# Turning the third and fourth chunks' first layer norm on VectorE by way of DRAM, instead of on TensorE

## The chip, the cores and the metric

The kernel runs on one core of one Trainium2 chip. The metric is the device time in microseconds (us) of one execution; lower is better. Engines are named as in the profile: PE (TensorE, matmuls), PEld (its weight loads), ACT (ScalarE), DVE (VectorE), POOL (GpSimd), SP (SyncE, which issues all the DMAs here).

## What is computed

One transformer block with conditioned layer norms, in float32: 2048 tokens of 512 features, 32 heads of 16 in a linear attention, and a bilinear gated unit of 1376 hidden features.

```python
mod = (_silu(c) @ w_mod).reshape(c.shape[0], 6, 1, -1)
sa, ca, ga, sb, cb, gb = (mod[:, 0], mod[:, 1], mod[:, 2], mod[:, 3], mod[:, 4], mod[:, 5])
h = _layernorm(x, axis=-1) * (1 + ca) + sa
x = x + ga * _A_ref(h, A_wqkv, A_wo)          # linear attention
h = _layernorm(x, axis=-1) * (1 + cb) + sb
x = x + gb * _B_ref(h, B_w_gate, B_w_up, B_w_down)   # ((h w_gate) * (h w_up)) w_down
```

In the attention, phi(t) is t + 1 for t > 0 and exp(t) otherwise, plus 1e-6; the keys' phi(k) enters a sum over all tokens (phi(k) times v, and phi(k) alone, here called z), which all queries then read.

## The kernel before

The 2048 tokens are four chunks of four tiles; a tile is 128 tokens by 512 features, a chunk `ch` has the tiles 4 ch to 4 ch + 3. Every float32 matmul is made of three: each operand is split into a high part (a copy in the matmul's own format, made on ACT, sometimes on DVE) and a low part (what is left, a subtraction on DVE or POOL), and the products high-high, high-low and low-high are added up in PSUM. One product of a 128-token tile with a 512x512 weight is so twelve matmuls with 512 columns: four slices `k` of the features, three each.

The order of the instructions is written by hand; each engine works through its own list in order. The change lies in the first half, the key loop (`for i in range(NT)`, 16 passes, `ch, j = divmod(i, 4)`). Pass `i` issues, for PE: the key projection of tile i + 2 (`proj(i + 2, wk)`, L207 to L209), in passes 3, 4, 6 and 7 also a query projection (`proj(q, wq)`), and `t_tile(i)` (L373 to L375), which adds tile i's part to the sum over tokens. For the other engines it issues: `k_split_x(i + 1)` and `k_split(i + 1)`, the high and low parts of the normalised tile (`xh`, `xl`) and of phi of its keys (`kh`, `kl`) that the next pass's `t_tile` reads; `k_phi(i + 2)`, which makes phi out of the projection (two ACT instructions, L337 and L338, one DVE instruction, L341); `z_add`; and a part of side work (`extra[i]`): the splits of the value weights, the modulation vectors (`mod_load`, `mod_part`), the splits of the output weights `wo_s`.

A projection needs the chunk's layer norm transposed, features on the partitions. Before, chunk `ch + 1` is made so while chunk `ch` runs: statistics in the last two passes of the chunk before (DVE, L242, L243; the power on POOL, L263), the normalised tiles (`xhat`, ACT, L272), then in passes j = 0 and j = 1 the transposes (`turn_x`: sixteen times 128x128 on PE against an identity, in two groups of eight a chunk, L293), and the reading of PSUM with scale and shift (`modulated`, ACT, L305) with the high part cast on DVE (L313) and the low part (L316). For the third and fourth chunks these groups stand in passes 4, 5, 8 and 9, each in the middle of `t_tile`.

After the loop the sum over tokens is scaled (L655, L656), split (L194, L195), multiplied with the value weights and then with the output weights (`w_out`).

In the second half the kernel already moves tiles through DRAM and turns them on DVE: `move_out` and `move_in` (one write of 128x512, four reads of 32x4x128), `turn_v` (L736), and for the last layer norm `flip` (L901) and `flipped` (L907). A DVE transpose turns blocks of 32x32; the DRAM pass regroups the blocks so that the whole is transposed.

All tiles of 128x512 come from one pool of 94 buffers; PSUM has eight banks, four of which (`bank`) serve the projections and the turns.

Of the kernel before, what the change touches and what calls it, by code (L numbers as in the profile page):

```python
# [8 lines left out]
F32 = mybir.dt.float32  # L9
F32R = mybir.dt.float32r  # L10
AF = mybir.ActivationFunctionType
ALU = mybir.AluOpType
AX = mybir.AxisListType

P = 128
NB = 94
BL = 32
NQ = P // BL
# [6 lines left out]
def tile_adaln_block(  # L25
# [12 lines left out]
    nc = tc.nc  # L38
    ctx.enter_context(tc.manual_schedule())
    _, S, D = x.shape  # L40
    F = w_gate.shape[1]
    KD = D // P
    NJ = 4
    CH = NJ * P
    NCH = S // CH
# [22 lines left out]
    def f32(ap):  # L68
        return ap.bitcast(F32)
# [3 lines left out]
    def T(p, tag, shape=(P, D), dt=F32, bufs=None):  # L73
        cnt[0] += 1
        return p.tile(list(shape), dt, tag="t" if p is tiles else tag, name=f"{tag}_{cnt[0]}", bufs=bufs)

    def B(tag, shape=(P, D), dt=F32):

        return T(tiles, tag, shape, dt)
# [4 lines left out]
    def bank():  # L84
        return T(ps_w, "bank")
# [20 lines left out]
    wide = consts.tile([P, NJ, D], F32, name="wide")  # L106
# [59 lines left out]
    def mod_col(acc, ps):  # L166

        for b in range(KD):
            nc.tensor.matmul(ps[:, b:b + 1], acc[:, b * P:(b + 1) * P], ones[:, 0:1], start=True, stop=True)
        return ps  # L170

    def col_out(v, ps, add):
        t = consts.tile([P, KD], F32, name=f"col{v}")
        nc.vector.tensor_scalar(t, ps[:, :KD], add, None, op0=ALU.add)
        return t
# [17 lines left out]
    def split(src, h, l, low=None):  # L193
        nc.scalar.activation(h, src, AF.Copy)  # L194
        (low or nc.vector).tensor_tensor(l, src, f32(h), op=ALU.subtract)  # L195

    def split_raw(raw, shape=(P, D), low=None):
        h = B("w", shape, F32R)
        l = B("w", shape, F32R)
        split(raw, h[:raw.shape[0]], l[:raw.shape[0]], low)  # L200
        return h, l
# [17 lines left out]
    def by_row(x):  # L219
        return x.rearrange("p (q s i) -> p s q i", q=NQ, i=BL)  # L220
# [96 lines left out]
                self.t[k] = (h, l)  # L317


    NT = NCH * NJ  # L320
    norm = [Norm(xts[0])]
    wk, wq, wv = [], [], []
    kx, phk, phq, q_ps = {}, {}, {}, {}

    def proj(i, w, of=bank):

        ch, j = divmod(i, NJ)
        ps = of()
        rows = w is wq and i not in FLIPPED
        product(ps.rearrange("p (s q i) -> p s q i", q=NQ, i=BL) if rows else ps,  # L330
                [(cut(norm[ch].t[k], j * P, (j + 1) * P), tuple(by_row(x) for x in w[k]) if rows else w[k])
                 for k in range(KD)])
        return ps
# [9 lines left out]
    def k_split_x(i):  # L343
        ch, j = divmod(i, NJ)
        kx[i] = [B("xh", dt=F32R), B("xl", dt=F32R)]
        split(norm[ch].n[j], *kx[i])

    def k_phi(i, ps):
        phi = B("phi")
# [11 lines left out]
    def k_split(i):  # L361
        h, l = B("kh", dt=F32R), B("kl", dt=F32R)
        phi = phk[i]
        nc.scalar.activation(h, phi, AF.Identity, bias=eps_phi)
        nc.vector.scalar_tensor_tensor(l, phi, EPS_PHI, f32(h), op0=ALU.add, op1=ALU.subtract)
        kx[i] += [h, l]

    def t_tile(i, *ks):
        xh, xl, kh, kl = kx[i]
        first, last = i == 0, i == NT - 1  # L370
        for k in ks:
            a, b = k * P, (k + 1) * P
            nc.tensor.matmul(tacc[k], xh[:, a:b], kh, start=first, stop=False)  # L373
            nc.tensor.matmul(tacc[k], xl[:, a:b], kh, start=False, stop=False)  # L374
            nc.tensor.matmul(tacc[k], xh[:, a:b], kl, start=False, stop=last)  # L375
# [6 lines left out]
    def q_b(i):  # L382
        phi_b(q_ps.pop(i), phq[i])
# [28 lines left out]
    ca = col_out(1, ps_ca, 1.0)  # L412
# [3 lines left out]
    sa = consts.tile([P, KD], F32, name="col0")  # L416
# [47 lines left out]
    nx = Norm(xts[1])  # L464
# [31 lines left out]
    rows, cols = {}, {}  # L496
    accs = {}

    raw_m, raw_o, wo_s = {}, [], []

    def mod_load(*vs):
        raw_m.update({v: load_mod(v) for v in vs})

    def mod_part(v, *ks):
        if 0 in ks:
            accs[v] = B("f")
        mod_acc(accs[v], raw_m[v], ks)
# [6 lines left out]
             9: lambda: (mod_part(2, 2, 3), mod_load(4)),  # L514
             10: lambda: (pairs.update({2: split_raw(accs[2], low=nc.gpsimd)}), mod_part(3, 0, 1, 2), raw_o.extend(load(wo_v[k], "raw") for k in range(2))),
             11: lambda: (mod_part(3, 3), mod_part(4, 0, 1), rows.update({2: mod_row(2, pairs[2])}), raw_o.extend(load(wo_v[k], "raw") for k in range(2, KD))),
             12: lambda: (mod_part(4, 2, 3), wo_s.extend(split_raw(x) for x in raw_o[:2]), cols.update({3: col_out(3, mod_col(accs[3], bank()), 0.0)}), mod_load(5)),
             13: lambda: (mod_part(5, 0, 1, 2), wo_s.extend(split_raw(x) for x in raw_o[2:]), cols.update({4: col_out(4, mod_col(accs[4], bank()), 1.0)})),
             14: lambda: (mod_part(5, 3),)}
    pairs = {}  # L520
    q_at = {3: 0, 4: 1, 6: 2, 7: 3}
    ahead = {2: k_ps[2], 3: k_ps[3]}
    turn_at = {4 * ch + j: (ch + 1, 2 * j, 2 * j + 1) for ch in range(1, NCH - 1) for j in range(2)}
    turn_at.update({1: (1, 0, 1), 2: (1, 2, 3)})
    for i in range(NT):
        ch, j = divmod(i, NJ)
        done = 0
        if i > 2:
            ahead[i + 2] = proj(i + 2, wk) if i + 2 < NT else proj(i + 6 - NT, wq)
        if i in q_at:  # L530
            qps = proj(q_at[i], wq)
        def turn_x():
            to, *ks = turn_at[i]
            nx.transpose(*ks)
            nx.modulated(ca, sa, *ks, cast=nc.vector)
            norm[to:] = [nx]

        fresh = i > 0 and ch + 1 < NCH and j == 0
        if i == 2:
            turn_x()  # L540
            wq.extend(split_blocks(r) for r in raw_q)
        if fresh:
            nx.xhat(2)
        if 0 < i < NT - 1:
            k_split_x(i + 1)
        if fresh:
            nx.xhat(3)
        if 0 < i < NT - 1:
            k_split(i + 1)
        if i in turn_at and i != 2:  # L550
            t_tile(i, 0, 1)
            done = 2
            turn_x()
        if i == 2:
            t_tile(i, *range(KD))
            done = KD
            ahead[i + 2] = proj(i + 2, wk)
        if ch + 2 < NCH and j == 2:
            nx2 = Norm(xts[ch + 2])
            nx2.stats(0, 1)  # L560
        if ch + 2 < NCH and j == 3:
            nx = nx2
            nx.stats(2, 3)
            nx.rstd_of()
            nx.nmr_of()
            nx.xhat(0, 1)
        if i + 2 < NT:
            k_phi(i + 2, ahead.pop(i + 2))
        else:
            q_a(i + 6 - NT, ahead.pop(i + 2))  # L570
            q_b(i + 6 - NT)
        if i in q_at:
            q_a(q_at[i], qps)
            q_b(q_at[i])
        if i + 1 < NT:
            z_add(i + 1)
        if i == NT - 2:
            pairs["z"] = split_raw(zacc, low=nc.gpsimd)
        if i == NT - 1:
            zps = row_sum(pairs["z"])  # L580
            zb = consts.tile([P, D], F32, name="zb")
            nc.scalar.activation(zb, zps, AF.Identity, bias=eps_z)
            zq = B("z")
            nc.gpsimd.tensor_copy(zq.rearrange("p (q s i) -> p q s i", q=NQ, i=BL), by_block(zb))
        t_tile(i, *range(done, KD))
        if i in extra:
            extra[i]()
    ga, sb, cb = rows[2], cols[3], cols[4]
# [64 lines left out]
    for k in range(KD):  # L653
        f = B("n")
# [62 lines left out]
    moved = {}  # L717

    def move_out(*tiles):

        for i in tiles:
            moved[i] = tc.dram_tile([P, D], F32, name=f"moved_{i}")
            nc.sync.dma_start(moved[i], phq.pop(i))

    def move_in(*tiles):

        for i in tiles:
            v = moved[i].rearrange("(m i) (q c) -> q i m c", i=BL, c=P)
            moved[i] = B("u")
            for q in range(NQ):  # L730
                nc.sync.dma_start(moved[i][q * BL:(q + 1) * BL].rearrange("i (m c) -> i m c", c=P), v[q])

    def turn_v(i):

# [163 lines left out]

    def flip(ch, *js):
        for j in js:  # L900
            nc.vector.transpose(wide[:, j].rearrange("p (m s i) -> p m s i", m=NQ, i=BL),  # L901
                                blocks.pop((ch, j)).rearrange("p (m s i) -> p m s i", m=NQ, i=BL))

    def flipped(ch, *ks):
        for k in ks:
            f = B("f")
            nc.scalar.activation(f.rearrange("p (x i) -> p x i", i=BL),  # L907
                                 wide.rearrange("p j (m s i) -> p (j m) s i", m=NQ, i=BL)[:, :, k],
                                 AF.Identity, scale=cb[:, k:k + 1], bias=sb[:, k:k + 1])
            blocks[ch, "f", k] = f  # L910

    stowed, blocks = {}, {}

# [518 lines left out]
```

## Time and profile before

| | |
|---|---|
| three runs | 553.96, 554.49, 555.14 us; median 554.49 |
| the profiled execution | 554.37 us, span of its instructions 552.7 us |
| busy share of the span | PE 99%, PEld 81%, DVE 68%, ACT 53%, POOL 37% |
| turns on PE in the whole run (L293) | 80 of 128x128, 10.4 us busy |
| DMA | 58.28 MB, mean 105 GB/s |

Times in the rows are microseconds from the span's start, means and durations in an instruction's row are marked there; a matmul's length in a row includes the time in which it overlaps the next one, so the pace is read from the starts. "xN" is a count of merged instructions; a bracket names the engine's idle time before the row and what ended it.

### The profile page before, as it was taken

The page shows a single profiled execution, that of the slowest core. Times are in us where ns is not written, and L with a number is a line of the kernel's source. Part 1 is how long each engine was busy: PE and PEld are TensorE (multiplying, and loading weights), DVE is VectorE, ACT ScalarE, POOL GpSimd, SP SyncE. Part 2 cuts the span into 40 slices and gives each one's busy share as a digit, 9 for nine tenths or more (in the row PEclk, how much of TensorE's full clock was granted, in tenths as well). Part 3 has the DMA queues.
Part 4 walks back from the last instruction along what each step waited for, and adds up shares of the span by engine and source line. Part 5 has one row for each costly group of instructions (what it writes and reads, how often), then busy time and mean ns, then how long its engine had stood idle before and what let it go on. Part 6 is the DMA issues. An engine that isn't in the chain of part 4 may idle for free.

```text
span 552.7 us, 7324 instructions
## 1 busy us (share of the span) xinstructions
PE 547.0 (99%) x2488; PEld 449.2 (81%) x2488; DVE 373.6 (68%) x610; ACT 291.7 (53%) x539; POOL 203.4 (37%) x204
## 2 busy tenths in 40 slices
PE   8999999999999999999999999999999999999997
PEld 7788888888888878878888888877888888888886
DVE  7896968986887886778776576985444444434434
ACT  3695856646476667566684545454443444444110
POOL 2000000102003201057596666766666546446200
PEclk9999999999999999999999999999999999999999
DMA  8900203320503205845545071690434222200004
GB/s 284 387 15 2 76 20 103 108 77 1 157 2 133 96 5 186 267 145 135 160 111 155 0 230 38 216 322 2 133 116 132 59 57 59 58 20 0 1 0 152
DMA packets 58373, 58.28 MB, mean 105 GB/s; under 512 B 7328, under 2 KB 38304, under 8 KB 58336
## 3 DMA queue, kind: packets, MB, share of 16 engines
q1 hardware_dynamic: 58336, 57.83, 33.2%
q8 instruction: 19, 0.31, 0.2%
q14 instruction: 18, 0.15, 0.1%
HBM read 42.60 MB, written 15.20 MB: 105 GB/s over the span
## 4 chain that ended last, share of the span: by engine, by line
PE 99%; DVE 0%; issue 0%
PE bank L1030 33%; PE acc L766 7%; PE acc L1110 6%; PE acc L1111 6%; PE acc L1112 6%; PE bank L207 5%; PE bank L209 5%; PE bank L208 5%; PE acc L375 3%; PE acc L374 3%; PE acc L373 3%; PE bank L849 2%; PE bank L851 2%; PE bank L850 2%; PE acc L146 2%; PE bank L293 2%
## 5 line engine op out<-in xcount | busy, mean ns | idle before, releaser
L1030 PE MATMUL bank<-h,w 128*128 128x512 f32 (+1 forms) x798 | 184.7, 390 | 0.0
L1030 PEld LDWEIGHTS bank<-h,w 128*128 128x128 f32 (+1 forms) x798 | 148.4, 186 | 33.4 <-ACT bank L1035 0.7
L1035 ACT ACTIVATE bank<-bank 128x512 f32<-128x512 f32 (+1 forms) x38 | 22.2, 583 | 139.6 <-PE bank L1030 139.5
L836 DVE TENSOR_TENSOR x<-acc,x 128x512 f32<-128x512 f32 (+1 forms) x73 | 48.8, 682 | 48.4 <-PE acc L1112 47.7
L1016 POOL TENSOR_TENSOR w<-raw,w 128x256 fp32r<-128x256 f32 (+3 forms) x38 | 40.9, 1077 | 91.0 <-ACT w L1009 91.0
L1111 PE MATMUL acc<-w,kh 128*128 128x512 f32 (+2 forms) x154 | 59.6, 387 | 0.0
L1110 PE MATMUL acc<-w,kh 128*128 128x512 f32 (+2 forms) x154 | 59.6, 387 | 0.0
L1112 PE MATMUL acc<-w,kl 128*128 128x512 f32 (+2 forms) x154 | 59.5, 386 | 0.0
L263 POOL TENSOR_TENSOR rstd<-ve,half 128x4 f32<-128x4 f32 (+1 forms) x10 | 11.0, 1103 | 121.8 <-DVE ve L262 69.6
L195 POOL TENSOR_TENSOR w<-raw,w 128x512 fp32r<-128x512 f32 (+1 forms) x25 | 35.1, 1409 | 52.2 <-ACT w L194 47.3
L1016 POOL TENSOR_TENSOR w<-t,w 128x512 fp32r<-128x512 f32 (+1 forms) x38 | 49.2, 1318 | 0.0
L195 DVE TENSOR_TENSOR kl<-u,kh 128x512 fp32r<-128x512 f32 (+1 forms) x38 | 26.4, 736 | 30.6 <-ACT kh L194 30.6
L207 PE MATMUL bank<-w,h 128*128 128x512 f32 x104 | 40.9, 394 | 0.0
L209 PE MATMUL bank<-w,h 128*128 128x512 f32 x104 | 40.6, 391 | 0.0
L208 PE MATMUL bank<-w,h 128*128 128x512 f32 x104 | 40.6, 390 | 0.0
L766 PE MATMUL acc<-w,xh 128*128 128x512 f32 x120 | 37.4, 393 | 0.0
L1089 DVE TENSOR_TENSOR u<-bank,u 128x512 f32<-128x512 f32 (+1 forms) x19 | 13.1, 691 | 31.6 <-PE bank L1030 25.1
L1110 PEld LDWEIGHTS acc<-w,kh 128*128 128x128 f32 (+1 forms) x154 | 28.9, 188 | 6.0
L1112 PEld LDWEIGHTS acc<-w,kl 128*128 128x128 f32 (+1 forms) x154 | 28.9, 188 | 5.9
L1111 PEld LDWEIGHTS acc<-w,kh 128*128 128x128 f32 (+1 forms) x154 | 28.9, 188 | 5.9
L998 POOL TENSOR_TENSOR t<-raw,t 128x256 f32<-128x256 f32 (+1 forms) x34 | 25.9, 761 | 1.4
L766 PEld LDWEIGHTS acc<-w,xh 128*128 128x128 f32 x120 | 22.2, 188 | 4.6
(211 smaller groups left out, 1116.5 us busy)
## 6 DMA issues: line engine op xcount, KB each, us to landing
raw<-in_w_mod_dram SPq DMA_DIRECT2D x24, 256.0 KB, 3.7
raw<-in_B_w_down_dram SPq DMA_DIRECT2D x20, 256.0 KB, 3.2
raw<-in_B_w_gate_dram SPq DMA_DIRECT2D x36, 128.0 KB, 3.4
raw<-in_B_w_up_dram SPq DMA_DIRECT2D x36, 128.0 KB, 3.4
x<-in_A_x_dram SPq DMA_DIRECT2D x16, 256.0 KB, 5.4
out_dram<-x SPq DMA_DIRECT2D x15, 256.0 KB, 2.6
raw<-in_A_wqkv_dram SPq DMA_DIRECT2D x12, 256.0 KB, 5.4
moved<-h SPq DMA_DIRECT2D x12, 256.0 KB, 2.1
```

Of the source, the lines that this page charges most:

```text
L195: (low or nc.vector).tensor_tensor(l, src, f32(h), op=ALU.subtract)
L207: nc.tensor.matmul(ps, ah, bh, start=i == 0, stop=False)
L208: nc.tensor.matmul(ps, ah, bl, start=False, stop=False)
L209: nc.tensor.matmul(ps, al, bh, start=False, stop=i == n - 1)
L766: nc.tensor.matmul(yps[i], x, y, start=False, stop=k == KD - 1 and x is al, skip_group_check=True)
L836: nc.vector.tensor_tensor(xt[:, a:b], dn[j][:, a:b], xt[:, a:b], op=ALU.add)
L998: sub = lambda out, x, y: (on or nc.gpsimd).tensor_tensor(out, x, y, op=ALU.subtract)
L1016: sub = lambda out, x, y: (on or nc.gpsimd).tensor_tensor(out, x, f32(y), op=ALU.subtract)
L1030: mm = lambda x, y, **kw: nc.tensor.matmul(ps, x[:, k], y, skip_group_check=True, **kw)
L1110: nc.tensor.matmul(ps, hh[:, a:b], dh[:n, c:d], start=i == 0, stop=False)
L1111: nc.tensor.matmul(ps, hh[:, a:b], dl[:n, c:d], start=False, stop=False)
L1112: nc.tensor.matmul(ps, hl[:, a:b], dh[:n, c:d], start=False, stop=i == len(hs) - 1)
```

## The change

The first layer norm of chunks 2 and 3 (the third and fourth) no longer goes over PE. In passes 3 and 7 all four tiles of the third and of the fourth chunk are normalised in regrouped order (`xhat_blocks`) and written to DRAM; in passes 4 and 8 each is read back in four pieces; in passes 5 and 9 DVE turns the four tiles into the constant buffer `wide`, and ACT makes a row of each k with scale and shift, followed by the high and low parts. For the third chunk, two of the four high parts are cast on DVE; for the fourth, all are on ACT. `k_split_x` reads the regrouped tiles of these chunks with strides. In pass 6 the query projection comes before the key projection. The four splits of the output weights move from passes 12 and 13 to 14 and 15. The helpers `lift_out`, `lift_in`, `lift_turn` and `lift_row` also take the place of the same instructions in the second half.

```diff
+    LIFTED = (2, 3)
+
+    def lift_out(name, x):
+        to = tc.dram_tile([P, D], F32, name=name)
+        nc.sync.dma_start(to, x)
+        return to
+
+    def lift_in(of):
+        v = of.rearrange("(m i) (q c) -> q i m c", i=BL, c=P)
+        u = B("u")
+        for q in range(NQ):
+            nc.sync.dma_start(u[q * BL:(q + 1) * BL].rearrange("i (m c) -> i m c", c=P), v[q])
+        return u
+
+    def lift_turn(j, u):
+        nc.vector.transpose(wide[:, j].rearrange("p (m s i) -> p m s i", m=NQ, i=BL),
+                            u.rearrange("p (m s i) -> p m s i", m=NQ, i=BL))
+
+    def lift_row(k, scale, shift):
+        f = B("f")
+        nc.scalar.activation(f.rearrange("p (x i) -> p x i", i=BL),
+                             wide.rearrange("p j (m s i) -> p (j m) s i", m=NQ, i=BL)[:, :, k],
+                             AF.Identity, scale=scale[:, k:k + 1], bias=shift[:, k:k + 1])
+        return f
+
+    def lift_parts(k, f, cast=True):
+        h, l = B("h", dt=F32R), B("h", dt=F32R)
+        if k % 2 and cast:
+            nc.vector.tensor_copy(h, f)
+        else:
+            nc.scalar.activation(h, f, AF.Copy)
+        nc.vector.tensor_tensor(l, f, f32(h), op=ALU.subtract)
+        return h, l
...
     def k_split_x(i):
         ch, j = divmod(i, NJ)
         kx[i] = [B("xh", dt=F32R), B("xl", dt=F32R)]
-        split(norm[ch].n[j], *kx[i])
+        if ch not in LIFTED:
+            split(norm[ch].n[j], *kx[i])
+            return
+        x = by_row(norm[ch].n[j])
+        h, l = (t.rearrange("p (s q i) -> p s q i", q=NQ, i=BL) for t in kx[i])
+        nc.scalar.activation(h, x, AF.Copy)
+        nc.vector.tensor_tensor(l, x, f32(h), op=ALU.subtract)
...
-             12: lambda: (mod_part(4, 2, 3), wo_s.extend(split_raw(x) for x in raw_o[:2]), cols.update({3: col_out(3, mod_col(accs[3], bank()), 0.0)}), mod_load(5)),
-             13: lambda: (mod_part(5, 0, 1, 2), wo_s.extend(split_raw(x) for x in raw_o[2:]), cols.update({4: col_out(4, mod_col(accs[4], bank()), 1.0)})),
-             14: lambda: (mod_part(5, 3),)}
+             12: lambda: (mod_part(4, 2, 3), cols.update({3: col_out(3, mod_col(accs[3], bank()), 0.0)}), mod_load(5)),
+             13: lambda: (mod_part(5, 0, 1, 2), cols.update({4: col_out(4, mod_col(accs[4], bank()), 1.0)})),
+             14: lambda: (mod_part(5, 3), wo_s.extend(split_raw(x) for x in raw_o[:2])),
+             15: lambda: wo_s.extend(split_raw(x) for x in raw_o[2:])}
...
-    turn_at = {4 * ch + j: (ch + 1, 2 * j, 2 * j + 1) for ch in range(1, NCH - 1) for j in range(2)}
-    turn_at.update({1: (1, 0, 1), 2: (1, 2, 3)})
+    turn_at = {1: (1, 0, 1), 2: (1, 2, 3)}
     for i in range(NT):
         ch, j = divmod(i, NJ)
         done = 0
+        up = ch + 1 if 0 < ch < NCH - 1 else None
+        if i == 6:
+            qps = proj(q_at[i], wq)
         if i > 2:
             ahead[i + 2] = proj(i + 2, wk) if i + 2 < NT else proj(i + 6 - NT, wq)
-        if i in q_at:
+        if i in q_at and i != 6:
             qps = proj(q_at[i], wq)
+        if up and j == 0:
+            lifts = [lift_in(x) for x in lifts]
+        if up and j == 1:
+            lift_turn(0, lifts[0])
...
-        if fresh:
-            nx.xhat(2)
         if 0 < i < NT - 1:
             k_split_x(i + 1)
-        if fresh:
-            nx.xhat(3)
-        if 0 < i < NT - 1:
             k_split(i + 1)
+        if up and j == 1:
+            lift_turn(1, lifts[1])
...
-            nx.xhat(0, 1)
+            nx.xhat_blocks(0, 1)
...
+        if ch + 2 < NCH and j == 3:
+            nx.xhat_blocks(2, 3)
+            lifts = [lift_out(f"first_{ch}_{n}", x) for n, x in enumerate(nx.n)]
...
         t_tile(i, *range(done, KD))
+        if up and j == 1:
+            lift_turn(2, lifts[2])
+            lift_turn(3, lifts[3])
+            for k in range(KD):
+                nx.t[k] = lift_parts(k, lift_row(k, ca, sa), cast=up == 2)
+            norm[up:] = [nx]
```

More of the change, by code (lines that the diff above doesn't have):

```diff
@@ L536, in turn_x @@
             norm[to:] = [nx]
-        fresh = i > 0 and ch + 1 < NCH and j == 0
         if i == 2:
@@ L721, in move_out @@
         for i in tiles:
-            moved[i] = tc.dram_tile([P, D], F32, name=f"moved_{i}")
-            nc.sync.dma_start(moved[i], phq.pop(i))
+            moved[i] = lift_out(f"moved_{i}", phq.pop(i))
     def move_in(*tiles):
         for i in tiles:
[L728 to L731, printed above, removed]
+            moved[i] = lift_in(moved[i])
     def turn_v(i):
@@ L900, in flip @@
         for j in js:
-            nc.vector.transpose(wide[:, j].rearrange("p (m s i) -> p m s i", m=NQ, i=BL),
-                                blocks.pop((ch, j)).rearrange("p (m s i) -> p m s i", m=NQ, i=BL))
+            lift_turn(j, blocks.pop((ch, j)))
     def flipped(ch, *ks):
         for k in ks:
[L906 to L910, printed above, removed]
+            blocks[ch, "f", k] = lift_row(k, cb, sb)
     stowed, blocks = {}, {}
```

## The prediction

> **What bounds it now.** I read the page first: the busy times, the chain that ended last, then the view of waits for the matmul engine (PE).
>
> ```profile
> PE 547.0 (99%) x2488; PEld 449.2 (81%) x2488; DVE 373.6 (68%) x610; ACT 291.7 (53%) x539; POOL 203.4 (37%) x204
> PE 99%; DVE 0%; issue 0%
> PE acc L146 <- DVE w L141: 2.0, 1, 2.0
> ```
>
> PE has one wait in the whole run, at the very start; the chain that ended last is PE alone. So a matmul taken out is worth its full length, and every wait that PE gets is paid in full. VectorE (DVE), ScalarE (ACT) and the DMA queue on SyncE (SP) are free only as long as what they make is there when PE arrives. The question is thus where PE stands, and where the other engines stand, in passes 4 to 10 of the key loop. The profiled execution took 554.37 us, 0.12 below the median of 554.49 and inside the runs' 553.96 to 555.14; I make the sum against it. The three runs lie within 1.2 us, so about 0.2% (1.1 us) is what can be told from no change.
>
> **What goes away.** From the chain (start, length), then PE's timeline (start, length, the instruction):
>
> ```profile
> 55.95 0.87 PE bank L293 x8
> ...
> 62.30 0.87 PE bank L293 x8
> ...
> 85.20 0.87 PE bank L293 x8
> ...
> 91.56 0.87 PE bank L293 x8
> ```
>
> ```profile
> 64.39 0.39 PE L207 MATMUL bank<-w,h 128*128 128x512 f32 x1
> ...
> 67.11 0.40 PE L207 MATMUL bank<-w,h 128*128 128x512 f32 x1
> ...
> 69.91 0.39 PE L373 MATMUL acc<-kh,xh 128*128 128x512 f32 x1
> ...
> 93.65 0.39 PE L207 MATMUL bank<-w,h 128*128 128x512 f32 x1
> ```
>
> The four groups of eight turns in passes 4, 5, 8 and 9 are the third and fourth chunks' (tiles 8-11 and 12-15): 4 x 0.87 = 3.48 us. Pass 6 starts at 64.39 with tile 8's key projection (2.72 us to 67.11) and then a query projection (2.80 to 69.91). With no wait, pass 6 would now start at 64.39 - 1.74 = 62.65; the change puts the query projection first, so the first matmul that needs the third chunk comes at 65.45. Pass 10 starts with tile 12's key projection and nothing in front of it: 93.65 - 3.48 = 90.17. These two are the due times.
>
> By the Trainium skill (VectorE: DVE Perf Modes, Rules for kernel authors) a 128x128 transpose belongs on TensorE when PSUM will do as its target, which speaks against this change; the same page (The three transpose paths) says that VectorE turns 32x32 blocks only, hence the way through DRAM. The page's 390 ns for one bf16 turn on TensorE would make 32 turns worth 12.5 us, an estimate, and the sum below 9.0 lower (552.3). The trace has 0.87 us for eight, and the sum goes by that.
>
> **What is added, third chunk.** The new way is serial: normalise four tiles (ACT), write them to DRAM, read each back in four pieces (SP), four turns (DVE), then per k a row with scale and shift (ACT), its high part and its low part. ACT as it ran:
>
> ```profile
> 50.15 1.52 ACT L272 ACTIVATE n<-x,nmr,rstd 128x512 f32<-128x512 f32 x2 [4.27 <-DVE nmr L267]
> 53.87 0.80 ACT L272 ACTIVATE n<-x,nmr,rstd 128x512 f32<-128x512 f32 x1
> 54.58 0.62 ACT L194 ACTIVATE xh<-n 128x512 fp32r<-128x512 f32 x1
> 55.10 0.80 ACT L272 ACTIVATE n<-x,nmr,rstd 128x512 f32<-128x512 f32 x1
> 55.81 0.71 ACT L364 ACTIVATE kh<-phi,eps_phi 128x512 fp32r<-128x512 f32 x1
> 56.43 1.45 ACT L305 ACTIVATE f<-bank,col,col 128x512 f32<-128x512 f32 x2
> 57.77 0.60 ACT L337 ACTIVATE phi<-bank 128x512 f32<-128x512 f32 x1
> 59.55 0.63 ACT L338 ACTIVATE h<-h 128x512 f32<-128x512 f32 x1
> ```
>
> The first rows stay. The third normalise starts at 53.87, the fourth now follows at once, at 54.58, and ends at 55.38; then xh at 55.29, kh at 55.81, and from 56.43 the four phi instructions. The last of these starts 59.55 - 57.77 = 1.78 later, at 58.21 (the row at 59.55 is the second exp), and ends at 58.84. What the new steps cost is shown by the same steps done elsewhere in the kernel:
>
> ```profile
> L736 DVE STREAM_TRANSPOSE f<-u x12: 668/704/711, 182.8 to 253.6; 128x512 f32<-128x512 f32 x12
> L907 ACT ACTIVATE f<-wide,col,col x8: 800/805/817, 302.8 to 345.7; 128x512 f32<-128x512 f32 x8
> L194 ACT ACTIVATE w<-raw x40: 508/622/638, 13.6 to 525.5; 128x512 fp32r<-128x512 f32 x36, 128x384 fp32r<-128x384 f32 x2, 96x512 fp32r<-96x512 f32 x2
> 181.77 3.72 SPq L731 DMA_DIRECT2D u<-moved  x8
> DMA to landing us min/median/max: 1.8/2.0/2.7
> 58.31 0.42 DVE L313 CAST h<-f 128x512 fp32r<-128x512 f32 x1
> 61.42 0.68 DVE L195 TENSOR_TENSOR w<-raw,w 128x512 fp32r<-128x512 f32 x1
> 62.02 0.69 DVE L195 TENSOR_TENSOR xl<-n,xh 128x512 fp32r<-128x512 f32 x1
> ```
>
> *SP.* It issues in order, 3.72 / 8 = 0.465 us each, so no read goes before the fourth write, which waits for the normalise that ends at 55.38. One write and fifteen reads later the last read is issued at 55.4 + 16 x 0.465 = 62.84 and lands 2.0 later, at 64.84 (this transfer's median; 2.7 is the worst seen).
> *DVE.* Instructions of this shape start 0.60 apart (61.42 to 62.02). Its order after the query's phi, which can start at 58.85, is: that phi, z, a low part of the value weights, turn 0, xl, kl, turn 1, phi, z, turn 2, turn 3. Ten later: turn 3 starts at 64.85, together with its data, and ends at 65.55.
> *Rows.* All four rows read all four turned tiles, so none starts earlier. ACT, in its order: row 0 65.6-66.4, its high part 66.4-67.05, row 1 66.95, row 2 67.65-68.45, its high part 68.5-69.1, row 3 69.0-69.8. DVE: low 0 at 67.1, high 1 (cast, 0.42) at 67.8, low 1 at 68.25, low 2 at 69.1, high 3 at 69.85, low 3 70.3-71.0. PE needs them in that order, waits from 65.45 to 67.1 for the first, crawls behind the rest and starts its last matmul of this projection at 71.05: done 71.3 and not 65.45 + 2.72 = 68.17. Wait: **3.1 us** against 1.74 saved.
>
> **Fourth chunk.** DVE goes on from low 3 (70.3) in this order: low part, xl, kl, two statistics, phi, phi, z, low part, xl, kl, two statistics, variance, the power on GpSimd, then the mean term (nmr) for which the normalising waits. Rows for the last of it:
>
> ```profile
> 68.73 0.69 DVE L242 BATCH_NORM_STATS2 st<-x 128x6 f32<-128x512 f32 x1
> 70.34 0.67 DVE L341 SCALAR_TENSOR_TENSOR phi<-bank,phi 128x512 f32<-128x512 f32 x1
> 74.41 0.69 DVE L242 BATCH_NORM_STATS2 st<-x 128x6 f32<-128x512 f32 x1
> 77.53 0.16 DVE L267 SCALAR_TENSOR_TENSOR nmr<-mv,rstd 128x4 f32<-128x4 f32 x1 [1.21 <-POOL rstd L263]
> ```
>
> Two statistics take 70.34 - 68.73 = 1.61; from the second pair's start to nmr it is 77.53 - 74.41 = 3.12. So 70.9 + 3 x 0.60 + 1.61 + 6 x 0.60 = 77.9, and nmr at 81.0, its end at 81.2. ACT: third normalise 53.87 - 50.15 = 3.72 after the first, 84.95; the fourth 0.71 on, ending at 86.5. SP: 86.5 + 16 x 0.465 = 93.95, landed 95.95. DVE gets to turn 3 at about the same time: ACT, after the fourth normalise, has two high parts (0.52 each), kh (0.62) and two phi instructions (0.63 each), so exp ends at 89.4, and DVE then has phi, z, two modulation parts, turn 0, xl, kl, turn 1, phi, z and turn 2 ahead of turn 3: 89.4 + 11 x 0.60 = 96.0; end 96.7. Row 0 ends at 97.55 and its high part at 98.2, where PE starts. Here every high part is on ACT, so row and high part follow each other at about 1.36 (0.83 for a row and the hop, 0.53 from a high part to the next): high 3 ends at 102.25, low 3 at 102.95, the last matmul is over at 103.25. PE came at 90.17 + 3.1 = 93.3 and would have been done at 96.0. Wait: **7.2 us**, 4.9 of it before the first matmul.
>
> **Small parts.** The strided reads (normalise by blocks, xh by rows) I cost at nothing more: the strided L907 takes the same 0.80 as L272. Behind the SP reads stand the loads of modulation weights of passes 6 and 8; their first readers are passes 8 and 10, so nobody waits. The turns' two PSUM banks come free; nothing waited for one. The output weights' split goes from passes 12 and 13 to 14 and 15: two high parts and two low parts now stand ahead of the last work before the key-value product.
>
> ```profile
> 127.89 2.41 ACT L655 ACTIVATE n<-acc,col 128x512 f32<-128x512 f32 x4
> 131.73 2.49 DVE L195 TENSOR_TENSOR w<-n,w 128x512 fp32r<-128x512 f32 x4
> 134.53 0.23 PE bank L209
> ```
>
> ACT's four come 1.05 later, and DVE's low parts, with 1.2 of added work and its wait for ACT, start at about 133.4: the fourth is ready at 135.9. PE starts the product at 134.76 and needs the fourth low part ten quarter-length matmuls on, 10 x 0.11 (as 0.87 / 8) = 1.1 later, at 135.9. Cost 0.1, cover just used up; a slip of DVE there would show one for one, so 0 to 1.
>
> **Sum.** 554.37 - 3.48 + 3.1 + 7.2 + 0.1 = 561.3. Unknowns: landing 1.8 to 2.7 twice, and hops between engines that I put at 0.03 to 0.05 (some ten in a row): +1.5 upward. Downward: the third chunk's wait cannot fall under about 1.5, since row and high part alone outpace PE's 0.69 per k; if the fourth's nmr kept its old lead over PE (93.65 - 77.53 = 16.1 less 1.74, against the 17.2 from nmr to the first high part), its wait would be 2.8 + 2.3 = 5.1: 554.37 - 3.48 + 1.5 + 5.1 = 557.5.
>
> **Rivals.** (1) *The old lead is kept*: 557.5, as just worked out. For it: nothing on DVE or ACT was late before. Against: DVE's count between 58.85 and 81 leaves it idle for only some 2 us.
> (2) *PE's clock falls in the wait of pass 10.* The trace has slow matmuls only after PE's idle start:
>
> ```profile
> 2.00 8.63 PE acc L146 x26
> ```
>
> 26 at 2.72 / 12 = 0.227 are 5.9 us, so this cold stretch cost 2.7. The same after 4.9 us of idling: up to 564.0. Against: PE crawls for 5 us anyway, which hides part of it. The Trainium skill (TensorE: Matmul & The Clock Gate, Part 1) states that an idle window of about 3.4 us halves the clock until a busy one; the start agrees, but the granted clock there still reads as full.
> (3) *Faster: the way through DRAM is done in time.* It decides at pass 10: nmr must come by about 73, 17.2 ahead of 90.17, and turn 3 of the third chunk by 63.8. Then all of 3.48 stays: 550.9. For it: ACT is busy for only 53% of the span, DVE 68%. Against: both are busiest here, and the serial part from nmr on (3.72 + 1.5 on ACT, 7.4 + 2.0 on SP, 0.7, 0.85, 0.65) is the rows' own. The changed order of passes 5 to 7 would have to free DVE by 8 us.
>
> **Chances.** Forecast (both waits) 0.55; (1) 0.15; (2) 0.18; (3) 0.10, and 0.02 that it ends within 0.2%. So faster 0.10, same 0.02, slower 0.88. The range runs from 556.5 (just under rival 1) to 565.5 (rival 2 and the unknowns upward); it leaves out (3) and a little on either side.
>
> **What would show it.** No L293 turns for tiles 8-15; a gap of PE at the first matmul of tile 8's key projection of about 1.6 us behind ACT's high part, then at tile 12's one of about 5, both named in PE's waits; rows of the new lift starting only when turn 3 ends; the last read of each chunk issued about 7.4 us after the fourth normalise. It is wrong if PE's waits are still only the one at the start, or if nmr of the fourth chunk comes long before 81.

## The result, and the profile after

| | before | after |
|---|---|---|
| runs | 553.96 to 555.72 us, median 554.82 (4 runs) | 563.06 to 564.66 us, median 563.72 (4 runs) |
| the profiled execution | 554.37, span 552.7 us | 563.73, span 562.0 us |

The changed kernel takes 1.0162 times as long, 95% interval 1.0143 to 1.0181. Two runs of the experiments below, one with the splits put back and one of before beside it, ran at a granted clock (the share of its full clock that PE was given) of 0.85 and 0.56 and are left out. The page of after, first PE's busy line, then the granted clock over the span, then the chain that ended last by engine:

```profile
PE 549.0 (98%) x2456; PEld 447.0 (80%) x2456; DVE 377.5 (67%) x612; ACT 295.7 (53%) x545; POOL 202.4 (36%) x204
PEclk9999999899999999999999999999999999999999
PE 78%; DVE 7%; ACT 6%; SPq 3%; DMA 3%; issue 1%; POOL 0%; POOLq 0%; ACTq 0%; DVEq 0%
```

The 32 turns are gone (2488 matmuls to 2456), and the chain that was PE alone now runs for a fifth of its length over the other engines. Where PE stood still, from the view of waits (us in total, times, longest), and PE's timeline at the two places:

```profile
PE bank L207 <- ACT h L351: 6.2, 2, 4.6
PE acc L146 <- DVE w L141: 2.0, 1, 2.0
PE acc L815 <- DVE xl L762: 0.8, 1, 0.8
PE bank L300 <- ACT n L272: 0.2, 1, 0.2
```

```profile
65.47 0.40 PE L209 MATMUL bank<-w,h 128*128 128x512 f32 x1
67.48 0.50 PE L207 MATMUL bank<-w,h 128*128 128x512 f32 x1 [1.61 <-ACT h L351]
...
69.24 0.63 PE L208 MATMUL bank<-w,h 128*128 128x512 f32 x1
69.67 0.63 PE L209 MATMUL bank<-w,h 128*128 128x512 f32 x1
...
72.27 0.39 PE L414 MATMUL acc<-kh,xh 128*128 128x512 f32 x1
...
98.90 0.63 PE L207 MATMUL bank<-w,h 128*128 128x512 f32 x1 [4.57 <-ACT h L351]
...
104.07 0.40 PE L414 MATMUL acc<-kh,xh 128*128 128x512 f32 x1
```

L351 is the high part of a row, L207 the first matmul of a key projection: the waits are those of tile 8 in pass 6 and of tile 12 in pass 10. After the wait PE crawls: each k has to wait for its own row and parts. From its first matmul to the next tile sum the projection of tile 8 takes 4.8 us and that of tile 12 5.2, where 2.7 is the length without waiting. Setting the same matmul of both kernels side by side gives the whole account:

| PE at | before | after | after minus before |
|---|---|---|---|
| first layer norm of the start | 12.95 | 13.21 | +0.26 |
| tile sum of pass 5, behind its turns (two groups gone) | 62.93 | 61.55 | -1.38 |
| end of the projections of pass 6 | 69.91 | 72.27 | +2.36 |
| tile sum of pass 9, behind its turns (two more gone) | 92.19 | 92.81 | +0.62 |
| end of the projection of pass 10 | 96.37 | 104.07 | +7.70 |
| in the key-value product | 135.66 | 143.72 | +8.06 |
| an output product of the second half | 251.68 | 260.76 | +9.08 |
| span | 552.7 | 562.0 | +9.3 |

In before the projection of pass 10 starts at 93.65 (quoted in the prediction) and the tile sum behind it here:

```profile
96.37 0.39 PE L373 MATMUL acc<-kh,xh 128*128 128x512 f32 x1
```

So 3.4 us are saved, pass 6 gives back 3.7, pass 10 gives back 7.1, and some 1.6 us come later. The fourth chunk's way to its first high part, in the timelines of DVE, ACT and SP and then in the chain of after (start, length, what; SPq is SP's DMA queue, `first` the copy in DRAM, `u` a tile read back):

```profile
81.51 0.16 DVE L267 SCALAR_TENSOR_TENSOR nmr<-mv,rstd 128x4 f32<-128x4 f32 x1 [1.21 <-POOL rstd L263]
81.71 1.52 ACT L279 ACTIVATE n<-x,nmr,rstd 128x512 f32<-128x512 f32 x2 [5.17 <-DVE nmr L267]
85.43 1.51 ACT L279 ACTIVATE n<-x,nmr,rstd 128x512 f32<-128x512 f32 x2
87.40 7.70 SPq L332 DMA_DIRECT2D u<-first  x16
95.76 0.70 DVE L336 STREAM_TRANSPOSE wide<-u 128x512 f32<-128x512 f32 x1
```

```profile
94.66 1.94 DMA u<-first
...
96.63 0.72 DVE wide L336
...
97.37 0.82 ACT f L341
...
98.22 0.64 ACT h L351
...
98.90 0.63 PE bank L207
```

The mean term comes at 81.5, 4.0 us later than in before (77.53, quoted in the prediction), and from ACT's normalising at 81.71 to the first row at 97.37 it is 15.7 us. The chain names the last read as the releaser of the fourth turn; but DVE had ended the third turn only at 96.46, so two queues arrive together, and which of them matters the chain can't say.

### The profile page after: what moved, and what is told of

The parts are those of the page before. It is cut to its first block, busy times and chain, and to the rows that moved or that the text cites. A ratio compares the mean times of both kernels' runs of the same rounds, so it can differ in the third digit from the quotient of the medians.

```text
span 562.0 us, 7353 instructions
## 1 busy us (share of the span) xinstructions
PE 549.0 (98%) x2456; PEld 447.0 (80%) x2456; DVE 377.5 (67%) x612; ACT 295.7 (53%) x545; POOL 202.4 (36%) x204
## 4 chain that ended last, share of the span: by engine, by line
PE 78%; DVE 7%; ACT 6%; SPq 3%; DMA 3%; issue 1%; POOL 0%; POOLq 0%; ACTq 0%; DVEq 0%
PE bank L1074 32%; PE acc L1154 6%; PE acc L1155 6%; PE acc L1156 6%; PE acc L815 6%; PE bank L207 3%; PE bank L209 3%; PE bank L208 3%; SPq L332 2%; ACT n L279 2%; PE bank L900 1%; PE bank L898 1%; PE bank L899 1%; DMA raw<-in_w_mod_dram 1%; DVE st L242 1%
## 5 line engine op out<-in xcount | busy, mean ns | idle before, releaser
L207 PE MATMUL bank<-w,h 128*128 128x512 f32 x104 | 43.0, 413 | 6.2 <-ACT h L351 6.2
L209 PE MATMUL bank<-w,h 128*128 128x512 f32 x104 | 42.0, 404 | 0.0
L208 PE MATMUL bank<-w,h 128*128 128x512 f32 x104 | 41.7, 401 | 0.0
L815 PE MATMUL acc<-w,xh 128*128 128x512 f32 x120 | 37.4, 393 | 0.0
L207 PEld LDWEIGHTS bank<-w,h 128*128 128x128 f32 x104 | 20.1, 193 | 12.2 <-ACT h L351 8.1
```

Of the source, the lines that this page charges most:

```text
L207: nc.tensor.matmul(ps, ah, bh, start=i == 0, stop=False)
L208: nc.tensor.matmul(ps, ah, bl, start=False, stop=False)
L209: nc.tensor.matmul(ps, al, bh, start=False, stop=i == n - 1)
L815: nc.tensor.matmul(yps[i], x, y, start=False, stop=k == KD - 1 and x is al, skip_group_check=True)
```

## The experiments

Theory: the two waits are the price, and both come from the time at which the serial way starts (the mean term, which DVE's list of work sets), so that the time from there to the rows decides. Rivals: the later splits of the output weights, the round trip through DRAM by itself, and the clock that falls in the waits. Ratios are to before, run on the same chip beside them.

**Splits of the output weights back in passes 12 and 13.**

```diff
+ 12: ... wo_s.extend(split_raw(x) for x in raw_o[:2]) ...
+ 13: ... wo_s.extend(split_raw(x) for x in raw_o[2:]) ...
- 14: ..., 15: ...
```

> Undoes one part: the output weights' splits go back to passes 12 and 13. Theory (the loss is two waits of PE, behind the third and the fourth chunk's rows, in passes 6 and 10): the waits stay, only the 0.3 us in front of the key-value product goes, so 563.4. Rival (the moved splits are a good part of the loss, since they stand ahead of the last work before that product): 2 us or more come back, 561.7 or less.

Median of three runs 562.59, ratio 1.0149 (1.0131 to 1.0167). The interval overlaps that of after. By the two ratios the place of the splits is worth 0.7 us, which the runs can't tell from nothing; the rival's 561.7 was not reached, the lowest run is 562.58. The 9 us are elsewhere.

**One chunk alone.** First only the third chunk by way of DRAM (`LIFTED = (2,)`, the fourth with turns on PE in passes 8 and 9), then only the fourth (`LIFTED = (3,)`, turns in passes 4 and 5, the key projection first in pass 6). In both the output weights' splits stay late.

> Only the third chunk goes through DRAM; the fourth is turned on PE as before. Theory: 1.74 us of turns saved, against a wait of 1.6 us and a crawl behind the rows of some 2 us in pass 6; no wait in pass 10: 2 us above before, 556.8. Rival (the loss is spread: strided reads, more DVE and ACT work, DMA traffic; half of it for each chunk): 559.3.

> Only the fourth chunk goes through DRAM; the third is turned on PE as before, and pass 6 has its old order. Theory: nmr of the fourth chunk comes at its old 77.5, the first high part 17.2 later at 94.7, PE is due at 93.65 - 1.74 = 91.9: a wait of about 2.8, a crawl of about 2.8, against 1.74 saved: 558.6, and the two single costs need not add up to the whole one, since the third chunk's delay of DVE is missing. Rival (spread loss, half for each chunk): 559.3, with no single wait of that size.

Third alone: 557.89, ratio 1.006 (1.0044 to 1.0076). Fourth alone: 559.30, ratio 1.0084 (1.0068 to 1.0101). Each is slower by itself. Waits of PE and the normalising of the fourth chunk, third alone:

```profile
PE bank L207 <- ACT h L351: 1.7, 1, 1.7
81.81 1.52 ACT L272 ACTIVATE n<-x,nmr,rstd 128x512 f32<-128x512 f32 x2 [4.92 <-DVE nmr L267]
```

and the same with the first row, fourth alone:

```profile
PE bank L207 <- ACT h L351: 3.0, 1, 3.0
77.72 1.52 ACT L279 ACTIVATE n<-x,nmr,rstd 128x512 f32<-128x512 f32 x2 [4.70 <-DVE nmr L267]
...
93.45 0.81 ACT L341 ACTIVATE f<-wide,col,col 128x512 f32<-128x512 f32 x1 [2.88 <-DVE wide L336]
```

It is the third chunk's way over DVE that pushes the start of the fourth's normalising from 77.7 to 81.8. From the normalising to the first row it is 15.7 us with the third chunk and without. The third's cost was expected a microsecond too low (557.9 against 556.8). In its trace pass 6 loses 4.1 us where 3.6 were expected, the excess in the crawl behind the rows above all; the execution also started 0.4 late (13.37 at the first line of the table, before 12.95), and 0.4 more come after pass 10.

**The round trip through DRAM left out.** This kernel omits the regrouping: the tiles are turned as they were normalised, so only the waits for DRAM and SP go.

```diff
- lifts = [lift_out(f"first_{ch}_{n}", x) for n, x in enumerate(nx.n)]
+ lifts = list(nx.n)
- lifts = [lift_in(x) for x in lifts]
```

> Leaves the DRAM pass out: DVE turns the normalised tiles themselves, so the blocks are not regrouped; everything else stays. Theory: DVE's own order is as late as the data (turn 3 of the third chunk stood there without a wait, that of the fourth waited 0.16 us for its data), so the rows come when they came and the time falls by 0.2 to 0.5 only: 563.3. Rival (the DMA round trip is the wait): turn 3 of the fourth chunk no longer waits for the reads, 4 to 5 us come back: 559.

Median 561.71, ratio 1.013 (1.0112 to 1.0148). Waits of PE and the fourth chunk's first row:

```profile
PE bank L207 <- ACT h L351: 6.2, 2, 4.7
96.23 0.81 ACT L341 ACTIVATE f<-wide,col,col 128x512 f32<-128x512 f32 x1 [4.56 <-DVE wide L336]
```

With no transfer at all the row comes 1.1 us earlier, and of that 0.7 is this execution's earlier start (12.49 at the first line of the table, after 13.21). The two waits stay as they were. So the DRAM path, named by the chain, is worth about 0.4 us; behind it stands DVE, which gets to its fourth turn no sooner. The 2.0 us by which the median is lower are, in the traces, that earlier start, these 0.4 and the late output product (L815), which this trace doesn't have.

**Two query projections ahead of the key projection in pass 6** (the query of pass 7 too), which gives the third chunk 2.8 us more.

```diff
- qps = proj(q_at[i], wq)
+ qps, qps_3 = proj(2, wq), proj(3, wq)
...
- qps = proj(q_at[i], wq)
+ qps = proj(q_at[i], wq) if i != 7 else qps_3
```

> Pass 6 gets both remaining query projections (tiles 2 and 3) ahead of the key projection that needs the third chunk, pass 7 none: 2.8 us more cover. Theory: the wait of pass 6 goes nearly whole (3.7 us of loss there become 0.4), but the fourth chunk's rows come when DVE's list lets them, at the same 97 us, so PE only waits longer in pass 10, by the same amount: 563.5, no gain. Rival (each wait stands for itself): 560.3.

Median 562.84, ratio 1.0144 (1.0131 to 1.0157). The wait of pass 6 is gone, and nothing is won by it:

```profile
PE bank L207 <- ACT h L351: 7.0, 1, 7.0
81.44 1.52 ACT L279 ACTIVATE n<-x,nmr,rstd 128x512 f32<-128x512 f32 x2 [5.47 <-DVE nmr L267]
```

PE comes earlier to pass 10 and waits longer there, since the normalising still starts at 81.44. The projection of pass 10 ends at 103.91, against 104.07 in after; the median is 0.9 lower, and of after's later waits that of the output product (L815, 0.8) is missing in this trace. The fourth chunk sets the end, at a time of its own; the third chunk's wait only takes part of it ahead.

**The fourth chunk earlier.** Its statistics go to pass 3, normalising and writing to pass 5, reading to pass 6, the turns to the end of pass 8, the rows to pass 9. The edit, shortened:

```diff
+ if ch == 0 and j == 3:  n4 = Norm(xts[3]); n4.stats(0, 1, 2, 3); n4.rstd_of(); ...; n4.nmr_of()
+ if i == 5:  n4.xhat_blocks(0, 1, 2, 3); lifts_4 = [lift_out(...) ...]
+ if i == 6:  lifts_4 = [lift_in(x) for x in lifts_4]
+ if i == 8:  lift_turn(n, lifts_4[n]) for n in range(NJ)    # at the pass's end
+ if i == 9:  n4.t[k] = lift_parts(k, lift_row(k, ca, sa)) for k in range(KD)
```

> The fourth chunk starts two passes earlier: its statistics in pass 3 (where DVE sat idle for 2.7 us), normalised and written in pass 5 (where ACT sat idle for 4 us), read in pass 6, turned at the end of pass 8, rows in pass 9. Theory: the wait of pass 10, 7.1 us of loss with its crawl, goes; that of pass 6 (3.7) stays: 556.6. Rival (the way through DRAM and DVE costs time wherever it stands): 561 or more.

Median 557.39, ratio 1.0046 (1.0031 to 1.0062). The waits for L351 are one of 1.8, in pass 6. That wait, the normalising of the fourth chunk, and PE at the start and the end of pass 10's projection:

```profile
PE bank L207 <- ACT h L351: 1.8, 1, 1.8
62.71 2.92 ACT L279 ACTIVATE n<-x,nmr,rstd 128x512 f32<-128x512 f32 x4
95.64 0.40 PE L207 MATMUL bank<-w,h 128*128 128x512 f32 x1
...
99.78 0.39 PE L414 MATMUL acc<-kh,xh 128*128 128x512 f32 x1
```

So the theory holds: with the same instructions the time falls by 6.3 us when the mean term comes early. In the traces pass 10 loses 1.4 (4.14 less 2.72) instead of 7.1.

**Both moves together, and with the third chunk left on PE.** The first is the early fourth chunk with two query projections in pass 6 and the output weights' splits in their old place; the second has the third chunk's turns on PE and the old order of pass 6.

> The early fourth chunk, both query projections ahead in pass 6, and the output weights' splits back in passes 12 and 13. Theory: no wait left but 0.4 us in pass 6, and the turns' 3.48 us are gained: 551.5. Rival (each wait that is taken away shows the next one, later): 554 or more.

> The third chunk is turned on PE as before, the fourth goes through DRAM early as in the kernel with the early fourth chunk; splits of the output weights in their old place. Theory: no wait of PE, 1.74 us gained: 552.8. Rival (the next wait shows): 554 or more.

Both moves: 552.98 (12 runs), ratio 0.9973 (0.9963 to 0.9983), faster than before, but short of the theory's 551.5 and better than the rival's 554. Third on PE: 555.29 (11 runs), ratio 1.0004 (0.9995 to 1.0013), no change; here the rival's number came out. Besides the 2.0 us at the very start neither trace has a wait of PE of over 0.6 us, and both lose 1.4 us in pass 10 (90.65 to 94.79 and 92.30 to 96.45, where 2.72 would do), where PE crawls behind the rows. First row of the fourth chunk and PE in pass 10, both moves together:

```profile
88.95 0.82 ACT L341 ACTIVATE f<-wide,col,col 128x512 f32<-128x512 f32 x1 [3.04 <-DVE wide L336]
```

```profile
90.65 0.40 PE L207 MATMUL bank<-w,h 128*128 128x512 f32 x1
...
91.65 0.50 PE L207 MATMUL bank<-w,h 128*128 128x512 f32 x1
...
92.72 0.39 PE L207 MATMUL bank<-w,h 128*128 128x512 f32 x1
```

A k takes 1.0 where three matmuls need 0.7. The second kernel is also 0.5 us behind before at 24 us, from the start: PE's granted clock from 15 to 20 us is 0.66 in its trace and 1.00 in before's. Its profiled execution took 554.48; why its median is 0.8 above that no trace shows.

**Rows earlier still.** The first of these two, with the four turns at the end of pass 7 and the rows at the end of pass 8.

> The version with the fourth chunk a pass cycle earlier, two query projections in pass 6 and the old place of the output weights' splits, in which the fourth chunk's four turns now go to the end of pass 7 and its rows and parts to the end of pass 8, one pass earlier each. Theory (what is left of the loss is the crawl of 1.2 us behind the rows in pass 10): the crawl is gone, PE starts tile 12's projection with all its parts there, and the time is 551.8 against 553.0 of the version before it. Rival (the rows' work, wherever it stands, delays the keys' parts or phi of the pass in which it stands by as much): a wait of about 1 us at the key sums of passes 9 or 10 instead, time 553 or more.

Median 551.49, ratio 0.9943 (0.9930 to 0.9955). Its normalising of the fourth chunk and its last row, and PE's start of pass 10:

```profile
61.95 2.92 ACT L279 ACTIVATE n<-x,nmr,rstd 128x512 f32<-128x512 f32 x4
...
88.36 0.80 ACT L341 ACTIVATE f<-wide,col,col 128x512 f32<-128x512 f32 x1
```

```profile
91.15 0.39 PE L207 MATMUL bank<-w,h 128*128 128x512 f32 x1
91.38 0.39 PE L208 MATMUL bank<-w,h 128*128 128x512 f32 x1
```

No crawl is left there; 3.0 of the 3.48 us stay. Pass 6 keeps one of 0.7: its key projection takes from 68.66 to 72.09. This is the best version, faster than both kernels.

**Filler matmuls in the waits.** The changed kernel, with 7 and 20 idle matmuls ahead of the projections of tiles 8 and 12.

```diff
+ for _ in range({8: 7, 12: 20}.get(i, 0) if w is wk else 0):
+     nc.tensor.matmul(ps, wk[0][0][:, :P], wk[0][0], start=True, stop=True)
```

> The changed kernel with idle matmuls put into PE's two waits: 7 ahead of tile 8's key projection and 20 ahead of tile 12's, written into the bank that the projection then starts afresh, so they add nothing to the result. At 0.23 us each they take 1.6 and 4.6 us, as long as the waits. Theory (the clock has a price of its own): the granted clock stays near 1.0 in both passes, the crawl runs at 0.23 us a matmul, the last three matmuls of each projection end some 0.6 us sooner, and the time is about 562.5 against 563.7. Rival (the low clock is hidden, since the rows set the pace of the crawl): the clock stays up all the same, but the time is 563.7, no change.

Median 563.30, ratio 1.0160 (1.0141 to 1.0180). PE in four stretches (stretch, its length, busy us and count, granted clock, DMA share, GB/s), first of after, then with the fillers:

```profile
65.00:70.00 5.00, 3.38 (x10) 0.84 0.62 204
70.00:75.00 5.00, 5.00 (x19) 0.82 0.00 0
...
95.00:100.00 5.00, 1.10 (x3) 0.91 0.82 236
100.00:105.00 5.00, 4.99 (x15) 0.75 0.59 219
```

```profile
65.00:70.00 5.00, 4.93 (x19) 1.00 0.59 202
70.00:75.00 5.00, 4.93 (x20) 1.00 0.00 0
...
95.00:100.00 5.00, 4.33 (x19) 1.00 0.85 237
100.00:105.00 5.00, 4.57 (x13) 1.00 0.58 220
```

```profile
71.87 0.39 PE L416 MATMUL acc<-kh,xh 128*128 128x512 f32 x1
...
99.14 0.50 PE L207 MATMUL bank<-w,h 128*128 128x512 f32 x1 [0.67 <-ACT h L351]
...
100.51 0.50 PE L207 MATMUL bank<-w,h 128*128 128x512 f32 x1
...
104.31 0.39 PE L416 MATMUL acc<-kh,xh 128*128 128x512 f32 x1
```

The clock stays up, and pass 6 ends at 71.87 (after: 72.27), but pass 10 at 104.31 (after: 104.07). From the first matmul of that projection on it is 5.17 us in both. There a row and its high part take 1.37 us a k (99.14 to 100.51), and three matmuls at the low clock 3 x 0.43 = 1.29: the low clock fits under the rows. The rival holds, but for 0.4 us in pass 6, where the rows come at the same times in both traces (first row at 65.95 and 65.96).

## Why the prediction was right, step by step

- *Turns gone.* 3.48 forecast; the table gives 1.64 and 1.74, 3.38. Right.
- *Third chunk.* The first high part was put at 67.1 and came at 67.4, the wait at 1.65 and 1.61. The crawl was mis-sized: 3.1 lost forecast, 3.7 measured. Of the missing 0.6 the fillers show 0.4 to be the clock, which I had given no price here; the rest is rows and low parts that come some 0.3 later. Without the DRAM pass the clock stayed at 1.00 in pass 6, and the same projection took 4.3 instead of 4.8.
- *Fourth chunk.* Mean term 81.0 forecast, 81.5 measured; fourth normalise over at 86.5, 86.9; last read landed 95.95, 96.60; fourth turn 96.0, 96.63; the wait before the first matmul 4.9, 4.57; end 103.25, 104.07. Every station is 0.4 to 0.8 late, and PE itself came 0.9 late (94.2, not 93.3); that the loss of 7.2 measured 7.1 is in part luck, since the two cancel. That the two waits aren't independent was in the sum already, since the second was counted from PE's delayed arrival; the two query projections showed it on the chip.
- *Splits of the output weights.* 0.1 forecast, 0.3 in the trace (7.74 at the pass 10 tile sum's end to 8.06), within the 0 to 1 given. The forecast read the product's start from the chain, 134.76, the end of the matmul before; in PE's timeline it starts at 134.59, so there was 0.2 less cover.
- *What the sum lacked.* Forecast and median differ by 2.4 us, and so do the profiled executions: 0.6 from pass 6, 0.2 from the splits, 0.3 from the start, 0.1 from turns less a little from pass 10, 0.3 at the end, and 1.0 in the second half, which no step had:

```profile
258.95 1.76 DVE L762 TENSOR_TENSOR xl<-f,xh 128x512 fp32r<-128x512 f32 x1 [1.18 <-ACT xh L758]
260.76 0.50 PE L815 MATMUL acc<-w,xl 128*128 128x512 f32 x1 [0.81 <-DVE xl L762]
```

 The subtraction took 1.76 us where the same one in before took 0.69 (at 249.50). This wait is in the traces of after and of the fourth chunk alone (0.6), and in none of the others; the order of the instructions there is the same. The subtraction began 0.07 after an addition of POOL (258.88, 1.27 long) and ended 0.56 after that one's end, as if it had waited for it. No run tests this, and why it fell so in these two traces is open.

- *Rival 1 (old lead kept, 557.5).* Its condition failed: the mean term was not at its old distance. Its price was right: with the fourth chunk alone the lead is the old one, and the wait was 3.0 where it says 2.8, the crawl 2.45 (94.97 to 100.14, less 2.72) where it says 2.3.
- *Rival 2 (the clock falls, 564.0).* The clock did fall, in both passes, and the time came within 0.3 us of the rival's. It still isn't the reason: with the clock held up the median is 0.4 lower, inside the scatter, and the ratios are 1.0160 and 1.0162. Its price of 2.7 was read from the kernel's start, where the granted clock is 1.00, so it was no price of the clock. A number that fits doesn't show a mechanism.
- *Rival 3 (done in time, 550.9).* The change didn't meet its condition. Met by hand (normalising at 61.95 in the last version, where about 73 was asked for the mean term; the third chunk covered by the second query projection), it gave 551.49. By the Trainium skill (VectorE: DVE Perf Modes, Rules for kernel authors) the 128x128 transpose belongs on TensorE when PSUM will do as its target; after agrees with it, and the last version doesn't: with the same turns on DVE, early enough, the kernel is 3.0 us faster than with them on TensorE.

## What to carry to other kernels

Work taken off the engine that bounds a kernel is won only if its replacement is ready when that engine arrives; so find the start of the replacement's serial chain (here the mean term, 15.7 us ahead of the first row) and compare it with the arrival, before counting what is removed. Where two queues reach a point together, the chain names one of them, and removing that one shows the other; removing an earlier wait of the bounding engine gains nothing while a later one is set by an absolute time. Here moving the start mended the step, while taking one of its parts out, the DRAM pass, won 0.4 us: the same instructions, begun a few passes earlier and with one more query projection ahead, turned 9 us lost into 3 us gained.

## What the runs showed of the hardware

- The granted clock can fall after a short wait: in after, 1.61 us of idling followed by a few scattered matmuls came before 0.84 and 0.82 in the two stretches of pass 6, with starts 0.43 apart instead of 0.23. It doesn't always: in the kernel without the DRAM pass a wait of 1.54 and the same crawl left it at 1.00. The Trainium skill (TensorE: Matmul & The Clock Gate, Part 1) puts an idle window at about 3.4 us; in after PE was idle for less than half of that at a stretch. Idle matmuls held it at 1.00.
- At the kernel's start the same instructions ran at a granted clock of 1.00 in the traces of before and after, and at 0.66 from 15 to 20 us in two others (fourth chunk early, with the third by way of DRAM and with it on PE), which cost PE about 1 us each. Why is open.
- DVE's subtraction `xl` of the second half (128x512) takes 0.66 to 0.69 us with POOL idle and up to 1.76 when it begins during an addition of POOL; it then ended some 0.55 us after that addition (after: 260.71 behind 260.15; fourth chunk alone: 256.63 behind 256.08; both moves: 243.66 behind 243.11). In before, at 249.50, it took 0.69, and POOL's two additions beside it 3.52, against 2.55 for two in after (250.27). That each waits for the other is a reading of these rows; no run tests it.
